# The last quarter of two V blocks, read in three transfers over 64, 32 and 32 partitions

## The chip, the cores and the metric

The kernel runs on one core of a Trainium2 chip. The core has TensorE (matmuls, "PE" in the profile, with its weight loads as "PEld"), VectorE ("DVE"), ScalarE ("ACT"), GpSimd ("POOL") and the queue of SyncE ("SP"), which here issues nearly all transfers. Sixteen DMA engines carry them out. The metric is device time in microseconds. The profile is one execution of the program; its span runs from the first to the last instruction, and the time of the execution is a little longer.

## What is computed

One decoding step for four sequences through four layers: attention, gated unit, attention, gated unit, all with residuals. Both attentions use the same weights and the same caches, and both gated units the same weights.

```python
W = min(4096, max(256, Sk // 4))          # 2048 of Sk = 8192
q = (x @ wq).reshape(B, Sq, Hq, Dh)       # B 4, Sq 1, Hq 32, Dh 128; 8 heads of K and V
k, v = k_cache[:, :, Sk - W:, :], v_cache[:, :, Sk - W:, :]
p = softmax(einsum("bhqd,bhkd->bhqk", q, k) * Dh ** -0.5)
attn = einsum("bhqk,bhkd->bhqd", p, v).reshape(B, Sq, Hq * Dh) @ wo
glu = (sigmoid(x @ w_gate) * (x @ w_up)) @ w_down        # 512 -> 1792 -> 512
x = x + attn(layernorm(x)); x = x + glu(layernorm(x))    # twice
```

Everything is bfloat16 in memory. K and V of the window are 2 MB a head and kind, 16 MB each over the eight heads.

## The kernel before, in words

The kernel is written as a list of operations, each with the engine that runs it, the pieces of memory that it reads and writes, and an estimated duration (`P.op`, L54). A planner (`_schedule`, L95) takes these estimates and fixes the order of work on TensorE, VectorE, ScalarE and GpSimd. SP issues its transfers in the order in which they are written down. A second pass (`_assign_sync`, L185) gives every operation the semaphore waits that it needs; the transfers use 32 semaphores in turn, so a transfer waits, before it is issued, for the one 32 places earlier. The order on each engine is then fixed: an instruction that waits holds up all behind it.

The planner counts a transfer at a latency and its bytes over a rate. The rate is chosen by the piece's size in `load_v`: 440 for 32 units, 430 for 16 units, 410 for others (`_TM`, L258).

On-chip memory is divided into units of 256 columns of bfloat16, that is 512 bytes in each of 128 partitions. `WHERE` (L413) says in which places each block lies. A V block has 32 units, or 16 KB in each partition. `v_d` (L332) lays the block of one head out as 32 groups of rows x 4 sequences x 8192 elements, so partition 4s + b holds group s of sequence b. The order of the dimensions on the DRAM side is therefore 32, 4, 8192.

The first attention (L998 to L1025) goes over the eight heads. For head h it issues wo of this head, V of this head, and K of head h+3. K is transposed on TensorE (`k_head`, L632, matmuls on L645) and copied back by ScalarE and VectorE (L655), and stays on the chip for the second attention. The scores are on L668, the softmax from L677 to L737, the product with V on L754 (`pv_wo`, L740; 64 matmuls a head), wo on L774 (heads 6 and 7) or L804. V blocks alternate between two places in the arena: V0_4 (layer 0, head 4) takes the upper one, which V0_2 leaves and V0_6 takes next. V0_7 comes in three transfers of 16, 8 and 8 units.

The second attention (L1039 to L1059) reads V again. From head 2 on, V2_h is put where K of head h-2 lay, as soon as the scores of that head are computed; V2_4 lies in place of K_2's block. It runs two heads ahead of the product with V. V2_0 to V2_3 and V2_5, V2_6 come in pieces as large as their places allow, V2_7 again in three.

The gated units (`glu`, L883) follow each attention: gate and up on L899, down on L963. Part of the weights is kept on the chip from one layer to the next. All transfers are issued by the one helper `dma` (L441, issue on L444), so the profile shows that line for all of them and tells them apart by their tensors.

The change touches `WHERE`, `load_v` (L451), which makes the transfers of a V block, and `pv_wo`, which consumes them.

Of the kernel before, what the change touches and what calls it, by code (L numbers as in the profile page):

```python
# [184 lines left out]
def _assign_sync(ops, order, n_dma_sems):  # L185
# [75 lines left out]
    bw_4k=410.0, bw_3k=406.0, bw_1k=355.0, bw_8k=430.0, bw_16k=440.0,  # L261
# [6 lines left out]
def build(nc, A_x, A_k, A_v, A_wq, A_wo, B_wg, B_wu, B_wd, out):  # L268
# [3 lines left out]
    NB, SQ, D = A_x.shape  # L272
    _, HKV, SK, DH = A_k.shape
# [15 lines left out]
    NR = NB * REP  # L289
# [4 lines left out]
    UNIT = 256  # L294
    NU = 75
    UBLK = BLK // UNIT
    UHEAD = NB * UBLK
# [34 lines left out]
    k_d, v_d = (a[:, :, SK - W:SK, :].rearrange("b h (s j) d -> h s b (j d)", j=NJ4) for a in (A_k, A_v))  # L332

    es = contextlib.ExitStack()
    with es:
        def sb(name, shape, dt):
            return es.enter_context(nc.sbuf_tensor(name, shape, dt))

        kt = sb("kt", [128, HKV * NB * BLK], BF16)
# [20 lines left out]
        rz = sb("rz", [128, NPT * NR], F32)  # L360
        pt = sb("pt", [128, NPT * NJ4 * NR], BF16)
# [28 lines left out]
        def blk_ap(s):  # L390
            return {"kt": kt, "ar": arena, "pt": pt, "pb": pb, "sx": side}[s[0]][:, s[1] * UNIT:(s[1] + s[2]) * UNIT]

        def blk_tok(s):
            return tuple((s[0], u) for u in range(s[1], s[1] + s[2]))
# [9 lines left out]
        MAIN = WKEEP[2][0][1]  # L404
        G0 = MAIN - KEEPG * GU

        def ar(u, n):
            return ("ar", u, n)
# [4 lines left out]
        WHERE = {}  # L413
# [14 lines left out]
        for h in range(2, HKV):  # L428
            WHERE["V2_%d" % h] = [("kt", (h - 2) * UHEAD + u, n)
                                  for u, n in (((0, 16), (16, 8), (24, 8)) if h == HKV - 1 else ((0, UHEAD),))]  # L430

        def bankb(b):
            return ps[:, b, :].bitcast(BF16)

        def c_dve(n, rate=None):
            return tm["dve_fix"] + n * (tm["dve_f32"] if rate is None else rate)
# [4 lines left out]
        def dma(name, dst, src, w, r=(), rate="bw_4k", nbytes=None, sem=None):  # L441
            if nbytes is None:
                nbytes = dst.partition_size() * dst.free_nbytes()
            o = P.op("sync", name, 0.0, lambda e, dst=dst, src=src: e.dma_start(dst, src),  # L444
                     r=r, w=w, dma_bytes=nbytes, dma_rate=tm[rate])
            if sem is not None:
                o.sem = sem
                o.inc = 16
            return o

        def load_v(L, h):  # L451

            got = []
            u0 = 0
            for s in WHERE["V%d_%d" % (L, h)]:
                n = s[2]
                dma("V%d_%d_%d" % (L, h, u0), blk_ap(s), v_d[h][:, :, u0 * UNIT:(u0 + n) * UNIT], w=blk_tok(s),
                    rate={32: "bw_16k", 16: "bw_8k"}.get(n, "bw_4k"), nbytes=128 * n * UNIT * 2)
                got.append((s, u0 * UNIT // 128))
                u0 += n  # L460
            return got

# [5 lines left out]
             r=[("ones_f",)], w=[("ident_f",)])  # L468
        P.op("gpsimd", "ident_b", 200.0, lambda g: g.tensor_copy(ident_r[:, :].rearrange("p (r x) -> p r x", r=4),
                                                                   ident_f[:, :].unsqueeze(1).broadcast_to([128, 4, 128])),  # L470
             r=[("ident_f",)], w=[("ident_b",)])
# [9 lines left out]
        def e_rowq(v):  # L481
            with nc.allow_low_precision("zeros and ones"):
# [7 lines left out]
             r=[("ident_f",)], w=[("perm",)])  # L490
        P.op("vector", "ofb", c_dve(128),
             lambda v: v.tensor_reduce(ofb[:, :], ident_f[:, :].rearrange("p (s b) -> p b s", b=NB), AXX, ALU.add),
             r=[("ident_f",)], w=[("ofb",)])
        P.op("vector", "ofr", c_dve(128),
             lambda v: v.tensor_reduce(ofr[:, :], ident_f[:, :].rearrange("p (r y) -> p r y", r=REP), AXX, ALU.add),
             r=[("ident_f",)], w=[("ofr",)])
# [4 lines left out]
             r=[("rowq",)], w=[("tin",)])  # L501
# [5 lines left out]
             r=[("tin",), ("tout",)], w=[("tout",)])  # L507
        P.op("vector", "same2", c_dve(32),
             lambda v: v.tensor_scalar(same[:, :], tout[:, :], -1.0e30, 1.0e30, ALU.mult, ALU.add),
             r=[("tout",)], w=[("same",)])  # L510
# [12 lines left out]
        def emit_xT_in(t):  # L523
            last = None
            for c in range(NC):
# [4 lines left out]
             w=[("psx",)], banks=(MB,))  # L530
        P.op("vector", "xT_cp", c_dve(NX), lambda v: v.tensor_copy(xT[:, :], bankb(MB)[:, 0:NX]),
             r=[("psx",)], w=[("xT",)], banks=(MB,))
# [207 lines left out]
        def pv_wo(L, n, h, pbk, pieces, prev=()):  # L740
            k2 = n % 2
            kp = n % NPT
            obk = pbk[k2]
            for s, j0 in pieces:
                def e_pv(pe, s=s, j0=j0):
                    last = None
                    for j in range(j0, j0 + s[2] * UNIT // 128):

                        q, c, tv = j // NJ, j % NJ // CB, j % CB
                        w0 = (kp * NJ4 + (tv * NB + q) * NCH + c) * NR  # L750


                        odd = w0 // NR % 2
                        last = pe.matmul(ps[:, obk, NR * (1 - odd):NR * (3 - odd)],  # L754
                                         blk_ap(s)[:, (j - j0) * 128:(j - j0 + 1) * 128],
                                         pt[:, w0 - odd * NR:w0 + (2 - odd) * NR],
                                         start=(j == 0), stop=(j == NJ4 - 1), skip_group_check=True)
                    return last
                prev = [P.op("tensor", "PV%d_%d_%d" % (L, h, j0), s[2] * UNIT // 128 * tm["pe_pair"], e_pv,
                             r=blk_tok(s) + blk_tok(("pt", kp * NR // 4, NR // 4)), w=[("pso", obk, j0)], banks=(obk,), order=prev)]  # L760
            ov = onb[:, k2 * NR:(k2 + 1) * NR]
            P.op("vector", "omul%d_%d" % (L, h), c_dve(NR),
                 lambda v: v.tensor_tensor(ov.rearrange("p (r b) -> p b r", r=REP),  # L763
                                           ps[:, obk, NR:2 * NR].rearrange("p (b r) -> p b r", b=NB),
                                           rz[:, kp * NR:(kp + 1) * NR].rearrange("p (b r) -> p b r", b=NB), ALU.mult),
                 r=[("pso", obk, j0) for _, j0 in pieces] + [("rz", kp)], w=[("on", k2)], banks=(obk,))

            o0 = 4 * NR
            if n >= NWR:
                def e_wo(pe):  # L770
                    last = None
                    for c in range(NC):
                        for r_ in range(REP):
                            last = pe.matmul(ps[:, obk, o0 + c * NB:o0 + (c + 1) * NB],  # L774
                                             wo_sb[:, h * WOH + r_ * D + c * 128: h * WOH + r_ * D + (c + 1) * 128],
                                             ov[:, r_ * NB:(r_ + 1) * NB],
                                             start=(c == 0 and r_ == 0), stop=(r_ == REP - 1), skip_group_check=True)
                    return last
                P.op("tensor", "WO%d_%d" % (L, h), tm["pe_pair"] * NC * REP, e_wo,
                     r=[("wo", h), ("on", k2)], w=[("psl", obk)], banks=(obk,))  # L780
                residual("w_acc%d_%d" % (L, h), ps[:, obk, o0:o0 + NX], [("psl", obk)], obk, L == 2 and n == HKV - 1)
                return

            def e_sel(pe):
                last = None
                for j in range(4):
                    last = pe.matmul(ps[:, obk, o0 + j * NR:o0 + (j + 1) * NR],
                                     ident_r[:, :].rearrange("p (x j) -> p j x", j=4)[:, j, :],  # L790
                                     ov, start=True, stop=True, skip_group_check=True)
                return last
            P.op("tensor", "sel%d_%d" % (L, h), tm["pe_pair"] * 4, e_sel,
                 r=[("on", k2), ("ident_b",)], w=[("psl", obk)], banks=(obk,))
            P.op("vector", "osel%d_%d" % (L, h), c_dve(4 * NR),
                 lambda v: v.tensor_tensor(onr[:, :].rearrange("p (j r b) -> p j r b", r=REP, b=NB),  # L796
                                           ps[:, obk, o0:o0 + 4 * NR].rearrange("p (j r b) -> p j r b", r=REP, b=NB),
                                           ofr[:, :].unsqueeze(1).unsqueeze(3).broadcast_to([128, 4, REP, NB]), ALU.mult),
                 r=[("psl", obk), ("ofr",)], w=[("onr",)], banks=(obk,))

            def e_wo(pe):
                last = None
                for j in range(4):
                    last = pe.matmul(ps[32 * j:32 * j + NR, WB, 0:D], onr[:, j * NR:(j + 1) * NR],  # L804
                                     wo_sb[:, h * WOH + j * D:h * WOH + (j + 1) * D],
                                     start=(n == 0), stop=(n == NWR - 1), skip_group_check=True)
                return last
            P.op("tensor", "WO%d_%d" % (L, h), 500.0, e_wo,
                 r=[("wo", h), ("onr",), ("psw0",)], w=[("psw", n)], banks=(WB,))
# [190 lines left out]
        pieces = []  # L1000
        for ktc in range(2):
            s = ("kt", HKV * UHEAD - (2 - ktc) * 2 * UBLK, 2 * UBLK)
# [30 lines left out]
        for ktc in range(2):  # L1033
            for w, q0, q1 in WHERE["q%d" % ktc]:
                dma("wq2_%d_%d" % (ktc, q0), blk_ap(w), wq_d[:, ktc, q0 * 128:q1 * 128], w=blk_tok(w),
                    rate="bw_8k" if q1 - q0 == HQ else "bw_4k")
# [11 lines left out]
        for n in range(2):  # L1048
            vs2[HEADS2[n]] = load_v(2, HEADS2[n])
# [12 lines left out]
        order = _schedule(P.ops, tm)  # L1062
# [59 lines left out]
```

## Time and profile before

| | |
|---|---|
| Median of 3 runs | 179.66 us (178.96, 179.66, 180.56) |
| Profiled execution: time, span, granted clock of TensorE | 179.73 us, 177.6 us, 0.788 |
| PE, PEld, DVE, ACT, POOL busy | 128.4, 100.8, 102.0, 57.6, 7.1 us |
| Read from DRAM | 70.00 MB, 394 GB/s over the span |
| V0_4 | issued at 59.71 us, landed at 79.96 |
| V2_4 | issued at about 131.6 us, landed at 149.51 |

A transfer's landing is the last of its sixteen completions, one from each DMA engine; the trace keeps the time of each, and the start, duration and size of each packet, but not the number of the DMA engine. For the transfers around the two blocks (us, in order of issue):

| Transfer | first completion | last | last - first |
|---|---|---|---|
| V0_0 | 33.74 | 35.75 | 2.01 |
| V0_3 | 66.89 | 68.90 | 2.01 |
| V0_4 | 77.95 | 79.96 | 2.01 |
| K_7 | 82.85 | 84.88 | 2.03 |
| V0_5 | 89.03 | 91.10 | 2.07 |
| V0_6 | 95.47 | 98.88 | 3.41 |
| V0_7, last of three | 101.92 | 105.47 | 3.55 |
| V2_3 | 142.23 | 144.49 | 2.26 |
| V2_4 | 147.12 | 149.51 | 2.39 |
| V2_5 | 152.02 | 154.41 | 2.39 |
| V2_6 | 156.92 | 160.47 | 3.55 |
| V2_7, last of three | 161.96 | 165.71 | 3.75 |
| last piece of w_down | 170.76 | 174.53 | 3.77 |

In the profile, "x64" is a count of instructions, "<-" stands between what is written and what is read or waited for, and "issue" is time in which an engine waited for nothing that the profile shows.

### The profile page before, as it was taken

The numbers are of one execution on the slowest core, as the hardware profiler recorded it, in microseconds if no ns is written. First come the engines' busy times: TensorE is split into PE (matmuls) and PEld (weight loads), VectorE is DVE, ScalarE is ACT, GpSimd is POOL, SyncE is SP. The second block draws the span as 40 slices with busy tenths as digits, with TensorE's granted clock in tenths as the row PEclk, the third lists the DMA queues.
The fourth block names the chain that finished last, engine by engine and source line by source line (L and its number), as shares of the span: only waits on it lengthen the run. The fifth ranks groups of instructions, "written<-read, shape, count | busy, mean of one in ns | idle before, by whom it ended". The sixth has DMA issues, their size and how long they took to land.

```text
span 177.6 us, 5778 instructions
## 1 busy us (share of the span) xinstructions
PE 128.4 (72%) x2640; PEld 100.8 (57%) x2640; DVE 102.0 (57%) x263; ACT 57.6 (32%) x80; POOL 7.1 (4%) x16
## 2 busy tenths in 40 slices
PE   0398649978978795767772657558659879957893
PEld 0397349767737665455661557448315556636783
DVE  6134246886587582976875232112299988958340
ACT  2064047864708465290744100300030311114000
POOL 5200000000000000000000002002000000000120
PEclk9999555996978999999999655555586996995555
DMA  5999999999999999999999999999999999999960
GB/s 196 413 424 435 406 439 435 421 408 446 417 428 410 423 434 428 410 435 418 417 415 379 392 377 407 408 368 360 415 433 435 428 432 421 428 403 405 414 271 10
DMA packets 10755, 70.36 MB, mean 396 GB/s; under 512 B 1128, under 2 KB 2412, under 8 KB 7276
## 3 DMA queue, kind: packets, MB, share of 16 engines
q1 hardware_dynamic: 10724, 70.00, 95.8%
q8 instruction: 20, 0.33, 0.7%
q14 instruction: 3, 0.02, 0.0%
q10 hardware_dynamic: 8, 0.00, 0.0%
HBM read 70.00 MB, written 0.00 MB: 394 GB/s over the span
## 4 chain that ended last, share of the span: by engine, by line
DMA 59%; PE 18%; DVE 13%; SPq 4%; issue 3%; ACT 2%; ACTq 0%; DVEq 0%
DMA arena<-in_A_v_cache_dram 49%; PE ps L754 8%; DMA arena<-in_B_w_up_dram 5%; DMA arena<-in_A_wq_dram 5%; DVE pt L712 4%; PE ps L668 4%; SPq L444 4%; PE ps L899 2%; DVE pb L698 2%; ACT pb L690 2%; DVE nmz L677 1%; PE ps L963 1%; DVE pb L819 1%; DVE tout L683 1%; PE ps L774 1%
## 5 line engine op out<-in xcount | busy, mean ns | idle before, releaser
L655 ACT COPY kt<-ps 128x1024 bf16<-128x1024 bf16 x40 | 39.0, 1016 | 36.8 <-PE ps L645 25.5
L645 PE MATMUL ps<-ident_r,kt 128*128 128x128 bf16 x512 | 41.9, 246 | 9.1 <-DMA kt<-in_A_k_cache_dram 7.0
L645 PEld LDWEIGHTS ps<-ident_r,kt 128*128 128x128 bf16 x512 | 36.0, 112 | 15.6 <-DMA kt<-in_A_k_cache_dram 9.4
L655 DVE COPY kt<-ps 128x1024 bf16<-128x1024 bf16 x24 | 29.2, 1218 | 12.7 <-PE ps L645 12.7
L690 ACT ACTIVATE pb<-ps,nmz 128x512 bf16<-128x512 f32 x16 | 11.1, 691 | 51.4 <-DVE nmz L687 45.1
L668 PE MATMUL ps<-kt,qs 128*32 128x512 bf16 x256 | 21.5, 471 | 5.8 <-ACT pb L690 2.5
L754 PE MATMUL ps<-pt,arena 128*128 128x32 bf16 x578 | 16.4, 179 | 8.2 <-DMA arena<-in_A_v_cache_dram 7.8
L754 PEld LDWEIGHTS ps<-pt,arena 128*128 128x128 bf16 x578 | 15.5, 98 | 9.7 <-DMA arena<-in_A_v_cache_dram 9.2
L712 DVE TENSOR_TENSOR pt<-ps,ofbr 128x1024 bf16<-128x1024 f32 x16 | 19.5, 1216 | 0.3 <-PE ps L701 0.2
L677 DVE TENSOR_REDUCE nmz<-ps 128x1 f32<-128x512 f32 x16 | 11.0, 688 | 8.4 <-PE ps L668 8.4
L668 PEld LDWEIGHTS ps<-kt,qs 128*32 128x32 bf16 x256 | 6.3, 109 | 14.2 <-issue 4.4
L754 PE MATMUL ps<-pt,kt 128*128 128x32 bf16 x384 | 11.7, 182 | 2.8 <-issue 2.8
L754 PEld LDWEIGHTS ps<-pt,kt 128*128 128x128 bf16 x384 | 10.9, 100 | 3.4 <-issue 3.1
L698 DVE STREAM_TRANSPOSE pb<-pb 128x512 bf16<-128x512 bf16 x16 | 11.3, 707 | 2.4 <-ACT pb L690 2.1
L763 DVE TENSOR_TENSOR onb<-ps,rz 128x16 bf16<-128x16 f32 x16 | 2.7, 170 | 16.5 <-PE ps L754 15.2
L899 PE MATMUL ps<-xn,arena 128*128 128x5 bf16 (+1 forms) x210 | 8.3, 173 | 2.6 <-DMA arena<-in_B_w_up_dram 1.0
L899 PEld LDWEIGHTS ps<-xn,arena 128*128 128x128 bf16 x210 | 8.1, 118 | 3.2 <-DMA arena<-in_B_w_up_dram 1.2
L588 POOL TENSOR_TENSOR rs<-pt,rs 128x4 f32<-128x4 f32 x4 | 4.1, 1013 | 120.2 <-DVE pt L584 120.2
L920 ACT ACTIVATE pt<-pt 128x56 f32<-128x56 f32 x2 | 0.5, 250 | 25.2 <-DVE pt L915 25.2
L557 PE MATMUL ps<-pt,nmz 128*128 128x4 f32 x16 | 4.6, 358 | 3.0 <-DVE pt L559 2.1
L701 PE MATMUL ps<-pb,perm 128*128 128x256 bf16 x16 | 5.1, 316 | 2.1 <-DVE pb L698 2.0
L804 PE MATMUL ps<-wo_sb,onr 128*16 128x512 bf16 x48 | 4.8, 388 | 2.3 <-DVE onr L796 1.2
(97 smaller groups left out, 108.4 us busy)
## 6 DMA issues: line engine op xcount, KB each, us to landing
kt<-in_A_k_cache_dram SPq DMA_DIRECT2D x8, 2048.0 KB, 24.6
arena<-in_A_v_cache_dram SPq DMA_DIRECT2D x7, 2048.0 KB, 20.3
kt<-in_A_v_cache_dram SPq DMA_DIRECT2D x5, 2048.0 KB, 17.9
wo_sb<-in_A_wo_dram SPq DMA_DIRECT2D x8, 512.0 KB, 25.2
arena<-in_B_w_gate_dram SPq DMA_DIRECT2D x6, 448.0 KB, 8.4
arena<-in_B_w_up_dram SPq DMA_DIRECT2D x5, 448.0 KB, 8.0
kt<-in_A_wq_dram SPq DMA_DIRECT2D x2, 1024.0 KB, 10.1
arena<-in_B_w_down_dram SPq DMA_DIRECT2D x4, 512.0 KB, 13.8
```

The costliest lines, as they stand in the source:

```text
L444: o = P.op("sync", name, 0.0, lambda e, dst=dst, src=src: e.dma_start(dst, src), r=r, w=w, dma_bytes=nbytes, dma_rate=tm[rate])
L645: last = pe.transpose(bankb(bank)[:, (v * NB + q) * 128:(v * NB + q + 1) * 128], kt[:, c0:c0 + 128], ident_b[:, :])
L655: return (e.tensor_copy if ev == "vector" else e.copy)(to, fr)
L668: last = pe.matmul(ps[32 * b:32 * b + 32, sbk, 0:CB * 128], qs[:, q0:q0 + 32], blk_ap(kblk(h, b))[:, c * CB * 128:(c + 1) * CB * 128], sta ...
L677: lambda v: v.tensor_reduce(nmv, ps[:, sbk, 0:CB * 128], AXX, ALU.max, negate=True),
L690: o = a.activation(pbuf[:, :], ps[:, sbk, 0:CB * 128], ACTF.Exp, bias=gv, scale=1.0, accum_out=zv)
L698: P.op("vector", "ptr%d_%d" % (L, h), 650.0, lambda v: v.transpose(turned[:, :], pbuf[:, :]), r=[("pb", 0), ("pb", 1)], w=[("pb", 2), ("pb ...
L701: lambda pe: pe.matmul(ps[:, tbk, 0:CB * NQ].rearrange("p (j x) -> p j x", x=NCH * REP), perm[:, :], turned[:, :].rearrange("p (j x) -> p ...
L712: lambda v: v.tensor_tensor(ptv.rearrange("p (j b r) -> p j b r", b=NB, r=REP), ps[:, tbk, 0:CB * NQ].rearrange("p (j r) -> p j r", r=REP) ...
L754: last = pe.matmul(ps[:, obk, NR * (1 - odd):NR * (3 - odd)], blk_ap(s)[:, (j - j0) * 128:(j - j0 + 1) * 128], pt[:, w0 - odd * NR:w0 + (2 ...
L804: last = pe.matmul(ps[32 * j:32 * j + NR, WB, 0:D], onr[:, j * NR:(j + 1) * NR], wo_sb[:, h * WOH + j * D:h * WOH + (j + 1) * D], start=(n ...
L899: last = pe.matmul(ps[:, bank, fc * wid:(fc + 1) * wid], cols[:, fc - g0, :], xn[:, ktc * (NB + 1):ktc * (NB + 1) + wid], start=(ktc == 0 ...
```

## The change

V0_4 and V2_4 are each divided into 24 and 8 units. The 24 units are one transfer over all 128 partitions. The 8 units (4 KB in each partition) are three transfers, over partitions 0 to 63, 64 to 95 and 96 to 127. Since the partition is four times the group of rows plus the sequence, these read 16, 8 and 8 groups on the DRAM side. The first of the three stands for the piece of memory as before; the other two get names of their own and the same waits as the first. The product with V is in two parts, 48 matmuls that wait for the first transfer and 16 that wait for the other three. All other V blocks are read as before. In all, SP issues six transfers more, and the same bytes move.

```diff
+        WHERE["V0_4"] = [ar(MAIN - UHEAD, 24), ar(MAIN - 8, 8)]
+        WHERE["V2_4"] = [("kt", 2 * UHEAD, 24), ("kt", 2 * UHEAD + 24, 8)]
+        UNEVEN = {("V0_4", 24), ("V2_4", 24)}
...
             for s in WHERE["V%d_%d" % (L, h)]:
                 n = s[2]
-                dma("V%d_%d_%d" % (L, h, u0), blk_ap(s), v_d[h][:, :, u0 * UNIT:(u0 + n) * UNIT], w=blk_tok(s),
-                    rate={32: "bw_16k", 16: "bw_8k"}.get(n, "bw_4k"), nbytes=128 * n * UNIT * 2)
-                got.append((s, u0 * UNIT // 128))
+                cuts = [0, 64, 96, 128] if ("V%d_%d" % (L, h), u0) in UNEVEN else [0, 128]
+                toks, first = (), None
+                for p0, p1 in zip(cuts, cuts[1:]):
+                    tk = blk_tok(s) if p0 == 0 else (("part", L, h, p0),)
+                    o = dma("V%d_%d_%d_%d" % (L, h, u0, p0), blk_ap(s)[p0:p1, :],
+                            v_d[h][p0 // NB:p1 // NB, :, u0 * UNIT:(u0 + n) * UNIT], w=tk,
+                            rate={32: "bw_16k", 16: "bw_8k"}.get(n, "bw_4k"), nbytes=(p1 - p0) * n * UNIT * 2)
+                    first = first or o
+                    o.deps |= first.deps - {o}
+                    toks += tk
+                got.append((s, u0 * UNIT // 128, toks))
                 u0 += n
...
-            for s, j0 in pieces:
+            for s, j0, tk in pieces:
...
-                             r=blk_tok(s) + blk_tok(("pt", kp * NR // 4, NR // 4)), w=[("pso", obk, j0)], banks=(obk,), order=prev)]
+                             r=tk + blk_tok(("pt", kp * NR // 4, NR // 4)), w=[("pso", obk, j0)], banks=(obk,), order=prev)]
...
-                 r=[("pso", obk, j0) for _, j0 in pieces] + [("rz", kp)], w=[("on", k2)], banks=(obk,))
+                 r=[("pso", obk, j0) for _, j0, _ in pieces] + [("rz", kp)], w=[("on", k2)], banks=(obk,))
```

## The prediction

> **What bounds the kernel now.** I read the shares of the page first, then its DMA queues, then the chain of waits, then the last stage in the timeline of TensorE, and last the trace's packet and completion records.
>
> ```profile
> DMA  5999999999999999999999999999999999999960
> ...
> q1 hardware_dynamic: 10724, 70.00, 95.8%
> q8 instruction: 20, 0.33, 0.7%
> ...
> q10 hardware_dynamic: 8, 0.00, 0.0%
> ...
> DMA 59%; PE 18%; DVE 13%; SPq 4%; issue 3%; ACT 2%; ACTq 0%; DVEq 0%
> ```
>
> The transfers are busy in every slice but the first and the last two, and the chain is mostly DMA. By stage (columns: time; PE, weight load, DVE, ACT, POOL busy; granted clock; DMA share; GB/s):
>
> ```profile
> 59.00:80.00 21.00, 15.39 (x282) 11.31 (x279) 15.15 (x29) 11.69 (x17) 0.00 (x0) 1.00 1.02 427
> 128.00:150.00 22.00, 17.78 (x378) 10.47 (x371) 19.64 (x55) 4.67 (x12) 0.00 (x0) 0.81 1.02 431
> 150.00:175.00 25.00, 20.18 (x553) 16.93 (x549) 14.44 (x53) 3.67 (x7) 1.80 (x2) 0.70 0.88 359
> ```
>
> These are the stages in which the two changed blocks are fetched. All sixteen DMA engines are full; 427 GB/s over 16 is 26.7 GB/s each, and the packet records show the same: a 16,384-byte packet is followed by the next on its engine 0.607 us later, 27.0 GB/s.
>
> But the sixteen are not level. Each transfer posts sixteen completions, one an engine. At 17.8 us those of one transfer lie within 0.49 us. At V0_4 they run from 77.95 to 79.96: eight lie within 0.66 us of the first, eight between 1.08 and 2.01. At V2_4 (147.12 to 149.51) it is again eight up to 0.98 and eight from 1.07 to 2.40. What parts them is the q8 row: 20 instruction fetches of 16 KB, one engine each, 0.95 to 1.16 us a packet (the page: 0.7% of 16 x 177.6 us over 20 is 0.99). Each of the first eight fetches sends another engine back, the ninth (91.0 us) sends a late one back again, to 3.4: they go round **eight engines**, the fetch engines. The transfer is there when the last of these is done, and this last engine is never dry where it counts: the last completions of 2 MB blocks come at 134.65, 139.58, 144.49, 149.51, 154.41, and 2 MB at 430 GB/s is 4.88 us.
>
> ```profile
> 59.71 20.24 DMA arena<-in_A_v_cache_dram
> 79.96 0.05 issue
> 80.00 1.78 PE ps L754 x64
> 81.80 17.09 DMA arena<-in_A_v_cache_dram
> ...
> 164.66 1.09 PE ps L754 x34
> 165.75 0.62 PE ps L754 x16
> ```
>
> The chain holds V0_4 itself (issued 59.71, landed 79.96). At the end V2_7's last quarter lands at 165.71 and its sixteen matmuls start at 165.75; from there it is 11.9 us of fixed work to the span's end. So what the change does to the slowest DMA engine reaches the end almost one for one. The base is the profiled execution's 179.73 us (span 177.6 and 2.1 around it), which is the median 179.66 within 0.07.
>
> **Part by part.** Six transfers are added: each of the two blocks is read by 24 units over 128 partitions and 8 units over 64, 32 and 32.
>
> *Issues.* 3 x 0.54 us more on SP's queue a block (V0_4's issue row). Behind V0_4 are K_7 and one wo, behind V2_4 is V2_5, issued at 135.13, when the four issues from about 131.6 are over (133.9). All land 18 to 25 us after issue, so the delay is covered: nothing; without that cover 1.6 us each. TensorE gets up to three more waits a block, each a step of 0.02 to 0.05 us of "issue": nothing.
>
> *Finer pieces.* After the last landing only 16 of 64 matmuls are left, 1.78 x 3/4 = 1.3 us saved, and V0_6 can be issued at 80.5. It lands 17.1 us after issue behind full engines, so that gains nothing. V2_4's matmuls start at 152.05, 2.5 us after landing: nothing either. Shorter rows cost: V0_7, in three transfers, put 5.02 us between the first completions before and after it (96.90, 101.92), V0_5, in one, 4.92 (84.11, 89.03). Two more transfers 0.10, three 0.15, two blocks **+0.3 us**.
>
> *Shares of the engines.* The whole quarter is 32,768 bytes on each engine, 1.21 us. The 64-row piece is 16,384 on each, 0.61. How many engines a 32-row piece uses isn't shown for its shape; the nearest rows are x, four rows, in the q10 row as eight packets (four of data, four completions), and the output, 16 partitions but outermost dimension 4 on the DRAM side, four completions. All others, with 32 or more there, post sixteen. The 32-row pieces have 8 there, so I take eight engines, 4 rows = 16,384 bytes each, the same eight for both. These eight then carry 0.61 us more than before, the others 0.61 less. The Trainium skill (DMA: Bandwidth & Descriptors, Why a DMA increments its semaphore by 16 and not by 1) states the rule: the largest count up to 16 that divides the slowest dimensions of both sides; the two fours agree with it.
>
> *Where they write.* In a whole transfer each engine writes eight partitions of its own. In a 64-row piece sixteen engines write four each: two engines into what one served, and half the partitions untouched. Whether 27.0 GB/s belongs to the engine or to what it writes into, no row tells for certain. If to the engine, nothing is lost. If to the destination, two engines that meet there run at half pace. I take the destination: 27.0 holds to 1% on all engines whatever the source, and the fetch packets, with another destination, take 0.95 to 1.16 us for the same bytes on the same engines. Take a leading engine, a fetch engine behind it by a lead s that shares its destination, and let the 32-row pieces fall on the leading one. It writes 0.61 us alone, then 1.21 us where the late one is still busy, so the late one loses up to 1.21; then the late one's own 0.61 falls on the leader's place and loses 0.61; it is spared 0.61. Net: nothing for s up to 1.21, 2 x (s - 1.21) up to s = 1.82, **+1.21** beyond. At V0_4 late engines are at 1.08 to 2.01 and six of eight leaders within 0.11; whichever are paired, the last comes out 0.9 to 1.2 later: +1.0. At V2_4 the leads are like this or 0.6 shorter (the leaders lost 0.61 more than the others the first time): +0.3 to 1.2, I take +0.7.
>
> By the Trainium skill (SBUF — State Buffer, Door 1: The DMA port swizzle) partitions 0 to 63 reach 8 of 16 ports, 196 GB/s against 328 for 128 partitions at 1 MiB; as an estimate from its asymptotes the 512 KB quarter would take 2.4 us for 1.2, +2.4 us in all. No run here shows it yet.
>
> **Sum:** 1.0 + 0.7 + 0.3 = **+2.0 us**, 181.7; from 0.9 + 0.3 + 0.3 to 1.2 + 1.2 + 0.3, 181.2 to 182.4.
>
> **Rivals.**
> 1. *Levelling, faster.* The pace belongs to the engine, and the 32-row pieces fall on the eight that fetch no instructions. Each fetch engine is spared 0.61 us a block. For it: the skew is eight against eight, and two blocks shift 2 x 1.21 = 2.4 us between the halves, just what V2_4 shows (2.40). The first block's 0.6 moves everything after it. Of the second only 0.55 counts: V2_7's matmuls start at 164.06 for other reasons, and 64 take 1.77, to 165.83 where they end at 166.38 now. So -0.6 - 0.55 + 0.3 = -0.85: 178.9, between 178.5 and 179.5. It decides where meeting at a destination costs under 0.6 us a block. Its far bound is a full levelling, the last engine's 3.81 against a mean of 1.6 at the end: -2.2.
> 2. *The wrong eight.* The 32-row pieces fall on the fetch engines, which the records don't name. With the pace at the destination a late engine loses 0.61 + 1.21 by meeting and 0.61 by load, 2.4 a block: +3.6 (with short leads) to 5.2, 183.3 to 184.9. With the pace of the engine 2 x 0.61 + 0.3 = +1.5: 181.2.
> 3. *No unevenness:* the 32-row pieces use all sixteen engines. Then 0.3 us (180.0), or with meeting 0.61 twice a block, +2.7 (182.4).
>
> **How the numbers follow.** Forecast 0.42; levelling 0.23; the wrong eight 0.13 with meeting, 0.07 without; no unevenness 0.15, half each. The run-to-run spread of the kernel, 178.96 to 180.56, is about 1%, so 1% (1.8 us) is what one measurement tells from none: bounds 177.9 and 181.5. Slower: 0.28 of the forecast, 0.13, 0.02 and 0.07, 0.50. Faster: only levelling beyond its sum towards 177.5, 0.06. The rest, 0.44, is within 1%. The range holds levelling to most of the wrong eight, 178.5 to 184.0; outside are the far ends of these two, under 0.2.
>
> **What would show it.** Right: the transfer rows for V of 256 and 128 KB; GB/s under 400 in the slices where V0_4 and V2_4 land; V0_4's last completion about 1 us later than 79.96; V2_7's last matmuls after 167. The completions of a 32-row transfer number eight or sixteen, which settles rival 3. Levelling shows as a spread of completions near 1.4 us behind V0_4 in place of 2.0, with the pace at 27 GB/s; the wrong eight as a spread over 3 us. What would make it wrong beside these: an order of TensorE's or VectorE's work that the planner changes because it counts 24- and 8-unit transfers at another rate, which would show as a wait in front of L645 or L668 that isn't there now.

## The result and the profile after

The changed kernel takes 185.28 us (median of 4 runs, 184.34 to 186.37) beside 179.96 (4 runs, 178.96 to 180.56): ratio 1.0303, 95% interval 1.0225 to 1.0381. It is 5.3 us slower, where +2.0 was forecast. The profiled execution of the changed kernel, 186.37 us with a span of 184.6, is the longest of its four, so differences between the two profiles add up to 6.6 us, not to 5.3.

From the page of the changed kernel, the rows of the transfers in 40 slices of 4.6 us, the queues, and the chain by engine:

```profile
DMA  5999999999999999999999999999999999999940
GB/s 189 417 428 438 425 405 461 415 433 414 426 419 429 415 429 410 363 292 411 408 416 390 377 413 404 327 343 397 423 434 431 419 299 304 419 406 402 411 191 7
...
q1 hardware_dynamic: 11044, 70.00, 95.2%
q8 instruction: 20, 0.33, 0.7%
...
DMA 67%; SPq 14%; PE 8%; DVE 7%; issue 1%; ACT 0%; DVEq 0%; ACTq 0%
```

The DMA engines are as busy as before in every slice but the next to last, and the bytes are the same 70.00 MB. But in two places that had no dip before, slices 17 and 18 (74 to 83 us) and 33 and 34 (148 to 157 us), they move 292 to 363 GB/s. These are the places where V0_4 and V2_4 arrive. (SPq's share of the chain rises from 4 to 14% because the chain now reaches a transfer of w_down over SP's issues at 146 to 163 us, the longest of them 5.39 us. The kernel before has such an issue too, 7.89 us at 147.39, but off its chain; the DMA engines are full meanwhile.) By windows around them (time; PE, weight load, DVE, ACT, POOL busy; granted clock; DMA share; GB/s), first the changed kernel:

```profile
77.00:82.00 5.00, 2.05 (x59) 1.77 (x56) 1.22 (x1) 2.29 (x4) 0.00 (x0) 0.78 1.05 262
...
150.00:153.00 3.00, 2.96 (x79) 1.97 (x76) 2.94 (x9) 0.64 (x2) 0.00 (x0) 1.00 1.04 249
153.00:157.00 4.00, 1.26 (x45) 1.18 (x44) 2.88 (x6) 0.78 (x2) 0.00 (x0) 0.74 0.98 302
```

then the kernel before, where the same blocks arrive:

```profile
76.00:80.00 4.00, 2.52 (x36) 1.83 (x34) 2.87 (x5) 3.97 (x6) 0.00 (x0) 1.00 1.02 434
...
150.00:155.00 5.00, 4.59 (x120) 3.26 (x117) 4.80 (x15) 0.78 (x2) 0.00 (x0) 1.00 1.01 429
```

A share of 1.05 at 262 GB/s means that all engines have a packet in hand and each packet takes longer. The packet records say how much: from 77 to 82 us a 4,096-byte packet takes a median of 0.289 us where it takes 0.159 in quiet stretches, and a 16,384-byte packet 0.998 for 0.611.

The completions of the pieces and of the transfers that follow (us):

| Transfer | changed: number, first to last | before: first to last |
|---|---|---|
| V0_4, 24 units (before: whole) | 16, 76.79 to 79.90 | 77.95 to 79.96 |
| V0_4, 64 rows | 16, 77.73 to 80.83 | |
| V0_4, 32 rows | 8, 78.80 to 81.70 | |
| V0_4, 32 rows | 8, 80.07 to 82.87 | |
| K_7 | 16, 84.74 to 87.52 | 82.85 to 84.88 |
| V2_3 | 16, 145.09 to 147.64 | 142.23 to 144.49 |
| V2_4, 24 units (before: whole) | 16, 148.77 to 152.87 | 147.12 to 149.51 |
| V2_4, last 32 rows | 8, 151.74 to 156.39 | |
| V2_5 | 16, 157.53 to 161.05 | 152.02 to 154.41 |

The last engine is 2.64 us later at K_7 than before, 3.15 at V2_3, and 6.64 at V2_5: 2.6 us for the first block, 3.5 for the second. Not all of this stays: at V2_6 and at V2_7's last piece it is 5.46 and 5.27 us (165.93 for 160.47, 170.98 for 165.71), since in the kernel before the last engine falls back there (V2_6's completions spread over 3.55 us after V2_5's 2.39). The chain of waits and TensorE's timeline of the changed kernel show it reach the work (start, duration; in the timeline the idle time and its cause in brackets):

```profile
61.70 21.17 DMA arena<-in_A_v_cache_dram
82.87 0.14 issue
83.00 0.60 PE ps L766 x16
83.61 0.02 issue
83.62 17.15 DMA arena<-in_A_v_cache_dram
```

```profile
171.02 0.61 PE L766 MATMUL ps<-pt,kt 128*128 128x32 bf16 x16 [0.66 <-DMA kt<-in_A_v_cache_dram]
...
179.49 0.62 PE L975 MATMUL ps<-arena,pt 128*32 128x128 bf16 x16 [0.41 <-DMA arena<-in_B_w_down_dram]
180.73 0.62 PE L975 MATMUL ps<-side,pt 128*32 128x128 bf16 x16 [0.62 <-DMA side<-in_B_w_down_dram]
```

The chain now holds the last 32-row piece of V0_4, landing at 82.87, and its 16 matmuls. V2_7's last matmuls start at 171.02 in place of 165.75, again on the landing, and the last products wait for w_down too, which before were just fed in time (w_down's last piece lands at 181.32 us for 174.53).

### The profile page after: what moved, and what is told of

Read it like the earlier page. It is cut to its first block, busy times and chain, and to the rows that moved or that the text cites. A ratio compares the mean times of both kernels' runs of the same rounds, so it can differ in the third digit from the quotient of the medians.

```text
span 184.6 us, 5786 instructions
## 1 busy us (share of the span) xinstructions
PE 127.9 (69%) x2640; PEld 98.6 (53%) x2640; DVE 102.0 (55%) x263; ACT 57.5 (31%) x80; POOL 7.1 (4%) x16
## 4 chain that ended last, share of the span: by engine, by line
DMA 67%; SPq 14%; PE 8%; DVE 7%; issue 1%; ACT 0%; DVEq 0%; ACTq 0%
DMA arena<-in_A_v_cache_dram 48%; SPq L448 14%; DMA side<-in_B_w_down_dram 10%; DMA arena<-in_B_w_up_dram 5%; DMA arena<-in_A_wq_dram 4%; PE ps L766 4%; PE ps L680 2%; DVE pt L724 2%; DVE pb L710 1%; DVE nmz L689 1%; PE ps L975 1%; ACT pb L702 0%; DVE zd L739 0%; DVE tout L695 0%; PE ps L911 0%
## 5 line engine op out<-in xcount | busy, mean ns | idle before, releaser
L657 PE MATMUL ps<-ident_r,kt 128*128 128x128 bf16 x512 | 40.3, 240 | 7.6 <-DMA kt<-in_A_k_cache_dram 4.8
L657 PEld LDWEIGHTS ps<-ident_r,kt 128*128 128x128 bf16 x512 | 34.2, 109 | 13.7 <-DMA kt<-in_A_k_cache_dram 6.9
L680 PE MATMUL ps<-kt,qs 128*32 128x512 bf16 x256 | 20.5, 454 | 5.5 <-DVE kt L667 2.2
L816 PE MATMUL ps<-wo_sb,onr 128*16 128x512 bf16 x48 | 5.8, 470 | 1.8 <-DVE tin L693 0.8
L612 PE MATMUL ps<-xn,side 128*128 128x5 bf16 (+1 forms) x124 | 4.1, 167 | 3.5 <-DMA side<-in_A_wq_dram 3.2
```

Source lines behind the costliest of these rows:

```text
L657: last = pe.transpose(bankb(bank)[:, (v * NB + q) * 128:(v * NB + q + 1) * 128], kt[:, c0:c0 + 128], ident_b[:, :])
L680: last = pe.matmul(ps[32 * b:32 * b + 32, sbk, 0:CB * 128], qs[:, q0:q0 + 32], blk_ap(kblk(h, b))[:, c * CB * 128:(c + 1) * CB * 128], sta ...
```

## The experiments

The theory after the result: two DMA engines that write into the same share of the partitions run at half pace there (destination theory). Its rivals: the uneven loads (load theory), the finer pieces with more waits and another order of work, and a meeting on the DRAM side. All kernels are made from the changed one; each time stands beside the kernel before on the same chip.

**Whole rows.** The pieces of 24 and 8 units stay, without partial transfers.

```diff
-                cuts = [0, 64, 96, 128] if ("V%d_%d" % (L, h), u0) in UNEVEN else [0, 128]
+                cuts = [0, 128] if ("V%d_%d" % (L, h), u0) in UNEVEN else [0, 128]
```

> V0_4 and V2_4 keep the pieces of 24 and 8 units, but the 8 units are one transfer over 128 partitions; the order of work on TensorE, VectorE and ScalarE is that of the changed kernel. If the loss comes from engines that meet at a destination, or from uneven loads of the engines, it is gone: 180.0 to 180.3 us beside 179.96, GB/s over 420 where the two blocks land. If the finer pieces, the added waits of TensorE or the planner's other order cost it, most of the 5.3 us stays: 184 to 185.5.

Measured: 179.25 us beside 179.37, ratio 0.9994 (0.9980 to 1.0008). Its windows:

```profile
76.00:84.00 8.00, 6.69 (x137) 5.91 (x138) 5.91 (x13) 5.54 (x7) 0.00 (x0) 0.91 1.02 428
...
145.00:155.00 10.00, 8.55 (x212) 5.91 (x213) 9.70 (x27) 1.56 (x4) 0.00 (x0) 1.00 1.01 427
```

Nothing is lost with the same order of work on the compute engines. The division in 24 and 8 units and the planner's order are out; the whole loss comes with the three partial transfers. This kernel also lacks their four further issues and the waits on them; the third experiment below keeps these.

**Two halves.** Even loads, but engines meet.

```diff
-                cuts = [0, 64, 96, 128] if ...
+                cuts = [0, 64, 128] if ...
```

> The 8 units are two transfers, partitions 0 to 63 and 64 to 127. Each runs on sixteen engines, so all loads are as before the change, but each engine writes 16 KB into the other half. Destination theory: a late engine loses 0.61 us twice a block, 2.4 + 0.2 = 2.6 us in all, 182.6 (181.5 to 183.2), and GB/s falls under 350 where the blocks land. Load theory (the engines' own pace, uneven loads): nothing lost, 180.1.

Measured: 182.13 us beside 179.37, ratio 1.0162 (1.0123 to 1.0200), 342 and 370 GB/s in the two windows:

```profile
76.00:84.00 8.00, 6.73 (x127) 5.57 (x125) 4.60 (x12) 5.30 (x7) 0.00 (x0) 0.92 1.01 342
...
145.00:155.00 10.00, 7.90 (x217) 5.78 (x212) 9.42 (x26) 2.22 (x6) 0.00 (x0) 1.00 1.01 370
```

In the second window the rate does not fall under the 350 named, but that window of 10 us is longer than the stretch itself: over 76 to 80 us the rate is 288 GB/s, over 148 to 151 us 292. The time is as the destination theory has it. Uneven loads are not needed for a loss.

**The same loads at home.** The 32-row pieces lie where their engines also write in a whole transfer, if the eight engines of such a piece are those that serve partitions 0 to 63 there. The trace names no engines, so this is assumed and tested by what comes out.

```diff
-                cuts = [0, 64, 96, 128] if ...
+                cuts = [0, 32, 64, 128] if ...
```

> The cuts are 0-31, 32-63 and 64-127: the same eight engines get 48 KB and the others 16 KB, as in the change, but the eight now write 32 KB into the partitions that they serve in whole transfers and only 16 KB elsewhere; the other eight write nothing elsewhere (in the change 32 KB and 16 KB). Destination theory: a late engine among the eight loses 0.61 by load and 0.61 by meeting, 2.4 + 0.3 = 2.7 us in all, 182.7 (181.5 to 183.2), about half of the change's 5.3. Load theory: the loads are the change's, so the loss is the change's, 185.3.

Measured: 181.43 us beside 179.37, ratio 1.0134 (1.0095 to 1.0173): 2.1 us by the medians. The number and sizes of the pieces, the issues and the waits are those of the change, and by the theory the engines' loads too; only the rows are others, and with them the order of the pieces. That takes away more than half of the loss (the change's 5.3 and 5.9 us were measured on other chips). The completions show where: the first engine is done with V0_4's two 32-row pieces at 77.45 and 78.14 us, 0.69 apart, near the 0.61 that its 16 KB take alone; in the changed kernel at 78.80 and 80.07, 1.27 apart.

```profile
76.00:84.00 8.00, 4.85 (x104) 4.34 (x101) 3.24 (x9) 3.90 (x6) 0.00 (x0) 0.87 1.00 370
...
145.00:155.00 10.00, 8.17 (x199) 5.49 (x196) 9.18 (x27) 1.55 (x4) 0.00 (x0) 0.93 1.02 387
```

For comparison the same windows of the changed kernel:

```profile
76.00:84.00 8.00, 3.83 (x92) 3.41 (x90) 2.36 (x6) 3.29 (x5) 0.00 (x0) 0.74 1.03 310
...
145.00:155.00 10.00, 7.65 (x197) 5.32 (x190) 9.60 (x29) 2.34 (x6) 0.00 (x0) 1.00 1.05 324
```

The load theory, which asked for 185.3, falls as the sole cause.

**One block in halves.** Each engine writes four times the bytes of the two-halves piece into the other half, in one block only.

```diff
-        WHERE["V0_4"] = [ar(MAIN - UHEAD, 24), ar(MAIN - 8, 8)]
-        WHERE["V2_4"] = [("kt", 2 * UHEAD, 24), ("kt", 2 * UHEAD + 24, 8)]
-        UNEVEN = {("V0_4", 24), ("V2_4", 24)}
+        UNEVEN = {("V0_4", 0)}
...
-                cuts = [0, 64, 96, 128] if ...
+                cuts = [0, 64, 128] if ...
```

> Only V0_4 is cut, all of its 32 units into two transfers of 64 partitions; V2_4 is read whole. Loads are even. Each engine writes 64 KB into the other half, four times the two-halves piece. Destination theory: a late engine whose partner leads loses up to the whole block's time again where it belongs to the lower half, 1.8 + 0.6 + 0.6 + 1.8 = 4.9 us, and 1.3 us where it belongs to the upper: 184.8 if such a lower engine is the last, 181.3 if not. Load theory and a price per transfer: one transfer more, 180.1.

Measured: 185.11 us beside 179.37, ratio 1.0336 (1.0300 to 1.0373), +5.7 us.

```profile
74.00:84.00 10.00, 4.25 (x64) 3.35 (x61) 5.54 (x10) 5.52 (x7) 0.00 (x0) 0.88 1.03 224
```

Over 10 us the engines move 224 GB/s at a share of 1.03, half of the usual rate, and from 76 to 82 us a 16,384-byte packet takes a mean of 1.187 us for 0.611. Meeting costs about a factor of two. The expected 4.9 us is already the block's whole time (4.88 us) once more, all that a pair can lose by half pace on this block; the 0.8 us over it are not explained. Here the order of work on TensorE, VectorE and ScalarE is that of the kernel before.

**Halves with other rows of DRAM.** The same destinations, but each half reads every second group.

```diff
-                            v_d[h][p0 // NB:p1 // NB, :, u0 * UNIT:(u0 + n) * UNIT], w=tk,
+                            v_d[h][slice(p0 // 64, 32, 2) if p1 - p0 == 64 else slice(p0 // NB, p1 // NB), :, u0 * UNIT:(u0 + n) * UNIT], w=tk,
```

> As the kernel with V0_4 in two halves of 64 partitions, but each half reads every second group of rows in DRAM (0, 2, 4 ... and 1, 3, 5 ...) in place of the first and the last sixteen. V0_4's rows so stand in another order, which changes what head 4 of the first attention computes and no amount of work. If the engines meet at the destination, the loss is that of the halves, 185.1 us beside 179.3 (184.5 to 185.8), and 16 KB packets take 1.19 us. If they met at the DRAM side, where half the cache block lies, the loss is gone or changes by over 2 us: below 183.

Measured: 185.09 us beside 179.39, ratio 1.0319 (1.0274 to 1.0364); from 76 to 82 us a 16,384-byte packet takes a mean of 1.174 us.

```profile
76.00:84.00 8.00, 4.36 (x55) 3.73 (x53) 4.92 (x8) 5.32 (x7) 0.00 (x0) 0.90 1.03 227
```

With other addresses in DRAM the loss is the same (227 GB/s, where the halves have 225 in this window): which rows are read does not matter, and the destination is left as the place of meeting.

**Each block alone.** Only the named block keeps its entry in `WHERE` and `UNEVEN`, with the change's cuts.

```diff
-        UNEVEN = {("V0_4", 24), ("V2_4", 24)}
+        UNEVEN = {("V0_4", 24)}
```

> Only V0_4 (first attention) is read in 24 units and three partial pieces; V2_4 is one transfer again. Destination theory: a late engine among the eight that take the 32-row pieces loses 0.61 by load and 1.82 by meeting, 2.4 + 0.15 = 2.6 us, 182.0 beside 179.4 (181.0 to 182.6). If the two blocks add up, this and the second block alone make the change's 5.3 us together.

Measured: 181.75 us beside 179.20, ratio 1.0141 (1.0110 to 1.0171).

```diff
-        UNEVEN = {("V0_4", 24), ("V2_4", 24)}
+        UNEVEN = {("V2_4", 24)}
```

> Only V2_4 (second attention) is read in 24 units and three partial pieces; V0_4 is one transfer, and the order of work on VectorE and ScalarE is that before the change. Destination theory: 2.6 us again, up to 3.5 as the changed kernel's profile has between the last completions of V2_3 and V2_5: 182.0 to 183.0. A theory by which the loss of the second block stems from the first (the engines already spread further) expects under 1.5 here: below 180.9.

Measured: 182.06 us beside 179.20, ratio 1.0140 (1.0102 to 1.0178). And the change on the same chip:

> The changed kernel itself beside the one-block kernels, on the same chip: 184.7 to 185.3, the sum of the two single blocks' losses within 0.7 us.

Measured: 185.12 us beside 179.20, ratio 1.0312 (1.0262 to 1.0362), +5.9 us. The blocks alone give +2.55 and +2.86, 5.4 together: they add up within the 0.7 named, and the second needs nothing of the first. The rate falls only where the block is cut, in the first block's kernel at 76 to 84 us,

```profile
76.00:84.00 8.00, 5.23 (x113) 4.80 (x112) 3.36 (x8) 4.47 (x6) 0.00 (x0) 0.93 1.01 295
...
145.00:155.00 10.00, 8.90 (x214) 6.05 (x211) 8.55 (x27) 1.84 (x5) 0.00 (x0) 0.83 1.01 426
```

in the second's at 145 to 155:

```profile
76.00:84.00 8.00, 7.26 (x144) 5.92 (x140) 6.01 (x12) 5.45 (x7) 0.00 (x0) 0.92 1.01 427
...
145.00:155.00 10.00, 7.51 (x178) 5.00 (x179) 8.15 (x24) 1.56 (x4) 0.00 (x0) 0.87 1.02 309
```

**Cuts at partitions 16 and 32.**

```diff
-                cuts = [0, 64, 96, 128] if ...
+                cuts = [0, 16, 32, 128] if ...
```

> A look at which engines a piece uses. The 8 units are cut at partitions 16 and 32: DRAM dimensions outside are 4, 4 and 24 groups. By the rule that the count is the largest up to 16 that divides the outer dimensions of both sides, the completions are 4, 4 and 12 (96 partitions, 24 groups). If a piece used as many engines as it can fill up to 16, the last would have 16. Four engines carry 64 KB, eight 32 KB, four none: 182 to 186 us.

Measured: 4, 4 and 12 completions a block; 185.84 us in one run. The count goes by both sides' outer dimensions, not by what a piece could fill. Of the four engines, three complete V0_4's first piece within 0.23 us and one 2.60 later.

## Why the prediction was wrong

*What bounds the kernel* held: the transfers were the bound, and the loss of the last DMA engine passed to the end, 5.27 us of it at V2_7's last matmuls (171.02 for 165.75). The 11.9 us behind them were not fixed, though: in the changed kernel's profile they are 13.6, since the last products wait for w_down there (12.6 when the change was run again).

*Issues, waits, finer pieces* held, and the +0.3 us for shorter rows was too much: whole rows in 24 and 8 units cost nothing (0.9994), and with the further issues the DMA engines stay full (share 0.98 to 1.06 around the blocks). The planner did move work, which the prediction named as what might make it wrong: in the first attention some transposes and copies of K stand elsewhere on TensorE, VectorE and ScalarE. The whole-rows kernel has that order and loses nothing.

*Eight engines for a 32-row piece* held: eight completions, which ends rival 3. The rule of the Trainium skill (DMA: Bandwidth & Descriptors, Why a DMA increments its semaphore by 16 and not by 1), the largest count up to 16 that divides both sides' slowest dimensions, also gives the 12 of the 96-row piece.

*The pace belongs to the destination* held, and is now shown: half pace with even loads, at other DRAM addresses too, and more than half of the loss gone when the rows are moved. The Trainium skill (SBUF — State Buffer, Door 1: The DMA port swizzle) says that partitions 0 to 63 reach only 8 of the 16 ports; the trace of the block in halves agrees, 224 GB/s where whole blocks have 427 to 434.

*The step that failed* is the pairing: "let the 32-row pieces fall on the leading one". I took it that the eight engines of these pieces are either all leaders or all fetch engines. They are neither. In the changed kernel's profile the first 32-row piece of V0_4 completes at 0, 0.21, 0.55, 0.57 and 0.85 us after the first, and then at 1.93, 2.56 and 2.90: five leaders and three late ones. Two further profiles with this cut of V0_4 show five and three too (within 0.24 us and from 1.59 on when the change was run again, within 0.12 and from 1.63 on with the first block alone). With three late engines among the eight, the last engine pays the price that rival 2 worked out for them, 0.61 by load and 1.82 by meeting, 2.4 a block. The two blocks alone, +2.55 and +2.86, fit 2.4, not the forecast's 1.0 and 0.7. Rival 2 had 5.2 us for two blocks with the shorter rows, 184.9; measured were 5.3 and 5.9 (185.28 and 185.12). As the shorter rows cost nothing, 0.5 to 1.1 us beyond twice 2.4 is not explained. That the last engine is one of these eight is read from the order of the completions: K_7's last comes 4.65 us after the last of the second 32-row piece (87.52, 82.87), and K_7's first 4.67 after that piece's first (84.74, 80.07), while the last of the 64-row piece, which all engines take, was done at 80.83. The trace gives no engine numbers, so which engines these are is inferred, not seen.

*The price of meeting*, as the experiments' expectations worked it out, was right in its form and off in size, both ways: the halves of one block gave 5.7 us for 4.9, the two small halves 2.8 for 2.6, the pieces at home 2.1 for 2.7.

*Levelling*, the rival on the fast side, fell with the destination. By this account an engine that is spared load loses as much or more where another writes into its share, and whole rows at 0.9994 are as fast as any cut tried. That a cut in the engines' favour could pay while an instruction fetch holds one of them up was not tried.

*The range* was too narrow: it ended at 184.0, in the middle of rival 2, on a chance of 0.13 for it. The mixed case, which has rival 2's price as soon as one late engine is among the eight, was not among the cases at all.

## What to carry to other kernels

In a stream of transfers that fills all DMA engines, keep each transfer over all 128 partitions: a piece over 64 of them, or over 32 that other engines serve in whole transfers, sends two engines into one share, and there both run at half pace, in neighbouring transfers too. Where the end hangs on the last of sixteen engines, price a change by the worst pairing that the completions allow, not by groups that look whole. Look at GB/s beside the DMA share: here the share stayed at 1.0 while the rate fell by half.

## What the runs showed that I had not expected

The slowdown starts before the partial pieces do: the 24-unit transfer, over all partitions, spreads its completions over 3.11 us (76.79 to 79.90) where the transfer before it has 1.93, as one expects if its late engines already meet leaders that are in the small pieces: from 77 to 82 us its 12,288-byte packets take a median of 0.75 us, for 0.465 before 74 us. And the instruction fetches, 20 of 16 KB, set equal engines apart: in the kernel before two fetches have put two of the sixteen 1.85 and 2.01 us behind the first by 35 us (V0_0). By V0_4, after seven fetches, eight are 1.08 us or more behind, so the fetches do not account for the late engines quite one by one, as the prediction had it. The page gives these fetches a share of 0.7%; only the single completions show what they do.
